# A windowed attention and expert-attention kernel on one core: batch 0 masked on TensorE and loaded in halves, gate steps ordered by data only, set-up work on GpSimd, and a new hand-written order

## The chip, the core and the metric

The kernel runs on one core of a Trainium2 chip. The core has five engines that run their own instruction streams in order and meet at semaphores: TensorE (PE, with a separate stream of weight loads, PEld), VectorE (DVE), ScalarE (ACT), GpSimd (POOL) and SyncE (SP), which here only issues DMAs. The metric is the device time of one execution in microseconds (us). Three runs of the kernel before took 251.45, 252.59 and 254.32 us; the median is 252.59.

## The reference, cut to what matters

There are 8 batches of 576 tokens. Stage one is attention with 8 heads of 64 and a symmetric window of 32 tokens. Its output, with the heads side by side, is x (8 x 576 x 512). Stage two is a mixture of four causal single-head attentions on x, of which each token uses two, with weights from a softmax over the two largest gate logits.

```python
scores = scale * np.matmul(q, k.transpose(0, 1, 3, 2))
mask = np.abs(pos[:, None] - pos[None, :]) <= window
scores = np.where(mask, scores, -1000000000.0)
attn = np.exp(scores - scores.max(-1)); attn /= attn.sum(-1) + 1e-09
x = np.matmul(attn, v)                       # heads side by side: (8, 576, 512)
logits = x @ w_gate                          # 4 experts, the 2 largest kept
for e in range(E):
    q = x @ wq[e]; k = x @ wk[e]; v = x @ wv[e]
    a = causal_softmax(scale * (q @ k.T))
    out += gate[e] * (a @ v @ wo[e])
```

## The kernel before, in words

The whole program is a list of steps, `ORDER`, written out by hand (L25 to L115). A loop at L617 calls the function of each step in turn. A step `name:batch,...#engine@bank` issues its instructions on their engines, so the list fixes the order on every engine at once: PE, DVE, ACT, POOL and the DMA queue of SP each run their own share of the list, in order. `#1` is DVE, `#2` ACT, `#3` POOL, and `@` gives the PSUM banks (0 to 7).

For one batch b, with g the group of four heads, the steps are:

- `lq`, `lk` (L319) load q and k on SP. Part 3 is one DMA for a whole group, each partition holding 18 tokens in a row (`o=18`). Parts 0, 1 and 2 have two tokens per run and four DMAs, one for each head. `lv` (L344) loads V in five tiles of 128 tokens (the last has 64).
- `tq`, `tk` (L336) transpose on DVE.
- `vu`, `vl` (L356) copy V into tiles shifted by 64 tokens, on ACT or POOL.
- `sc` (L366) computes the scores of one group and one half of the columns on PE, in four banks; `ex` (L388) takes the exponential on ACT, two per `sc`; `mk` (L391) multiplies by the 0/1 mask on POOL, one after each `ex`.
- `av` (L398) multiplies by V on PE, and `un` (L418) divides by the row sums on DVE, with a buffer `RC` for the reciprocals. `xt` (L433) transposes x on PE, `xf` (L443) copies it out, `xb` (L453) makes a bf16 copy.
- `ga` (L459) is the gate's matmul. `gt` (L480), `gm` (L489) and `gu` (L497) are its small steps on DVE and `ge` (L486) its exponential on ACT; all four work in one PSUM bank.
- `pp`/`pe` are the q and k projections and their copies, `pv`/`ve` the same for v, `ps`/`xe` the expert scores and their exponentials, `se` the causal selection on POOL, `po`/`oe` the product with v and its scaling, `pt`/`ot` a transpose, `py`/`ye` the output projection, and `st` the store. `ye` and `st` use one of three buffers, chosen by the row tile, so `ye` of the next batch waits for the store of this one.

Set-up steps make the mask (`s_mask`, L239), the identity (`s_ident`), ones and zero paddings (`s_ones`, `s_padx`, `s_pade`, on DVE), load the expert weights (`lw`) and cast them (`cw`, L292, on DVE).

Two rules beyond data order the work. `touch` (L201) makes each instruction on a bank wait for the last instruction of every other engine on that bank, whatever bytes they use. `load` (L230) makes a DMA wait for the last PE instruction that stands before it in the list, so that loads are not begun too early.

## Time and profile before

| | us |
|---|---|
| median of three runs (lowest, highest) | 252.59 (251.45, 254.32) |
| the profiled execution, its own time | 251.16 |
| its span, first to last instruction | 249.50 |
| busy: PE, PEld | 219.0 (88%), 174.7 (70%) |
| busy: DVE, ACT, POOL | 168.6 (68%), 154.0 (62%), 147.2 (59%) |
| chain that ended last: PE, DMA, DVE | 66%, 13%, 11% |
| mean granted TensorE clock | 0.977 |

All durations in this document come from one profiled execution of 251.16 us. "Busy" is the union of an engine's instructions; a matmul's end is modelled, so a busy PE is not PE at its peak. In the timeline, a line gives the start, the length, the engine, the source line, the operation, what it writes and reads, and in brackets how long the engine had been idle before it and what ended that. A line number can be that of a helper: L225 and L224 are the copies on DVE or POOL and on ACT, L231 the loads, L478 the gate's small DVE operations, L328 the transposes of part 3, and L332 those of parts 0 to 2.

### The profile page before, as it was taken

What the parts mean: (1) busy time and instruction counts of PE and PEld (TensorE: products, weight loads), DVE (VectorE), ACT (ScalarE), POOL (GpSimd) and SP (SyncE); (2) the same over time, 40 slices, a digit from 0 to 9 for tenths busy, and PEclk for the clock granted to TensorE, in tenths of its full rate; (3) what the DMA queues carried; (4) which work ended last, traced back from release to release, by engine and by line L of the source; (5) the groups of instructions that cost most, each with busy time, mean ns of one, the idle gap of its engine ahead of it and who ended that gap; (6) DMA issues with size and microseconds to landing.
All of it is one profiled execution on the core that took longest, in us unless ns stands there. A gap on an engine that the chain in (4) does not pass through costs nothing.

```text
span 249.5 us, 12294 instructions
## 1 busy us (share of the span) xinstructions
PE 219.0 (88%) x5474; PEld 174.7 (70%) x5488; DVE 168.6 (68%) x360; ACT 154.0 (62%) x224; POOL 147.2 (59%) x171
## 2 busy tenths in 40 slices
PE   0485897999999999899999999995899999999963
...
PEclk9998899999999999999999999999799999999987
DMA  6995797779895976769936890689032212033166
GB/s 224 210 248 179 192 240 194 170 170 290 185 193 143 202 186 139 247 149 219 247 84 202 198 259 16 174 192 243 1 97 63 83 26 87 4 128 149 52 221 214
DMA packets 71446, 40.66 MB, mean 163 GB/s; under 512 B 46048, under 2 KB 64480, under 8 KB 71392
## 3 DMA queue, kind: packets, MB, share of 16 engines
...
## 4 chain that ended last, share of the span: by engine, by line
PE 66%; DMA 13%; DVE 11%; issue 4%; ACT 2%; SPq 2%; DVEq 0%; ACTq 0%
PE PS L404 13%; PE PS L381 12%; PE PS L516 8%; PE PS L528 7%; PE PS L597 6%; PE PS L437 5%; PE PS L546 5%; PE PS L573 5%; DMA qn<-in_q_dram 5%; DMA V<-in_v_dram 4%; PE PS L462 3%; DMA kn<-in_k_dram 2%; DMA out_dram<-Y 2%; SPq L231 2%; DVE Tkn L328 1%
## 5 line engine op out<-in xcount | busy, mean ns | idle before, releaser
L393 POOL TENSOR_TENSOR A<-A,MASKP 128x576 f32<-128x576 f32 x64 | 89.6, 1419 | 28.3 <-ACT A L389 26.8
L551 ACT ACTIVATE ATE<-PS 128x1024 bf16<-128x1024 f32 (+1 forms) x64 | 51.2, 838 | 23.1 <-PE PS L546 19.9
L389 ACT ACTIVATE A<-PS 128x576 f32<-128x576 f32 x64 | 38.7, 650 | 37.1 <-PE PS L381 36.5
L381 PE MATMUL PS<-Tqn,Tkn 32*64 32x128 f32 (+3 forms) x2560 | 47.8, 284 | 13.9 <-DVE Tkn L328 9.4
L381 PEld LDWEIGHTS PS<-Tqn,Tkn 32*64 32x64 f32 x2560 | 41.0, 140 | 20.2 <-DVE Tkn L328 9.8
L558 POOL TENSOR_SCALAR_AFFINE_SELECT ATE<-ATE 128x384 bf16<-128x384 bf16 (+2 forms) x64 | 26.1, 439 | 26.9 <-ACT ATE L551 26.6
L404 PE MATMUL PS<-V,A 128*64 128x65 f32 x1024 | 36.1, 228 | 3.7 <-POOL A L393 2.0
L404 PEld LDWEIGHTS PS<-V,A 128*64 128x64 f32 x1024 | 33.3, 143 | 7.1 <-POOL A L393 2.1
L225 POOL COPY V<-V 64x2112 f32<-64x2112 f32 (+1 forms) x10 | 18.1, 1813 | 18.7 <-DMA V<-in_v_dram 18.4
L328 DVE STREAM_TRANSPOSE Tqn<-qn 128x576 f32<-128x576 f32 x16 | 19.5, 1246 | 8.2 <-DMA qn<-in_q_dram 8.2
L328 DVE STREAM_TRANSPOSE Tkn<-kn 128x576 f32<-128x576 f32 x16 | 19.8, 1246 | 5.9 <-DMA kn<-in_k_dram 5.9
L423 DVE TENSOR_TENSOR XN<-PS,RC 128x512 f32<-128x512 f32 x32 | 22.1, 692 | 1.1
L597 PE MATMUL PS<-WO,OTT 128*128 128x512 bf16 x66 | 19.0, 409 | 3.3 <-ACT Y L224 1.9
L528 PE MATMUL PS<-WV,XTB 128*128 128x256 bf16 x160 | 21.5, 286 | 0.0
L516 PE MATMUL PS<-XTB,WQ 128*128 128x288 bf16 x128 | 18.0, 286 | 3.5 <-DVE OE L581 3.5
L516 PE MATMUL PS<-XTB,WK 128*128 128x288 bf16 x128 | 18.2, 286 | 0.8 <-DVE WK L295 0.8
L528 PEld LDWEIGHTS <-XTB 128*128 128x128 bf16 x160 | 16.1, 103 | 3.2 <-issue 0.2
L224 ACT CAST QKE<-PS 128x576 bf16<-128x576 f32 x19 | 12.1, 643 | 9.4 <-PE PS L516 9.4
L225 POOL CAST XTB<-XTF 128x128 bf16<-128x128 f32 (+1 forms) x19 | 10.3, 569 | 12.7 <-ACT XTF L224 8.6
L546 PE MATMUL PS<-QKE 64*128 64x64 bf16 (+4 forms) x192 | 17.1, 278 | 0.8 <-DVE QKE L225 0.7
L573 PE MATMUL PS<-VE,ATE 128*128 128x65 bf16 x480 | 17.3, 193 | 0.0
L573 PEld LDWEIGHTS <-ATE 128*128 128x128 bf16 x480 | 16.3, 97 | 1.2 <-POOL ATE L558 0.2
...
## 6 DMA issues: line engine op xcount, KB each, us to landing
...
```

The source lines that it names most:

```text
L225: return (nc.vector if engine == 1 else nc.gpsimd).tensor_copy(out_, in_)
L328: nc.vector.transpose(T.rearrange("q (p o) -> q o p", o=18), n_[:, :].rearrange("p (o d) -> p o d", d=64)[:, :, 32 * dh:32 * dh + 32])
L381: touch(nc.tensor.matmul(one(bank)[64 * par:64 * par + 64, lo - c0:hi - c0], KT[r, dh, k0:k0 + 64], QT[r, dh, lo:hi], start=(dh == 0), sto ...
L389: touch(nc.scalar.activation(a_part(b, g, half, p), two(b0)[:, :, 0:HS], EXP, scale=scale_att), b0, b0 + 1)
L393: nc.gpsimd.tensor_tensor(out=ap, in0=ap, in1=MASK[:, None, HS * half:HS * half + HS].to_broadcast([128, 2, HS]), op=MULT)
L404: touch(nc.tensor.matmul(one(b0 + h // 4)[64 * i:64 * i + 64, 65 * (h % 4):65 * (h % 4) + 65], A[:, h % 4, c:c + 64], V[:, slot, h, 0:65], ...
L516: touch(nc.tensor.matmul(one(b0 + half)[:, 0:HS], WQK[j][n][:, dt, :], XTB[b % 2][:, dt, HS * half:HS * half + HS], start=(dt == 0), stop= ...
L528: touch(nc.tensor.matmul(one(bank)[:, 256 * (t % 2):256 * (t % 2) + 256], XTB[b % 2][:, dt, 128 * t:128 * t + 128], WV[:, dt, :], start=(d ...
L546: touch(nc.tensor.matmul(one(b0 + eo)[:, at:at + hi - lo], Q[r, 1, 128 * kt:128 * kt + 128], Q[r, 0, lo:hi], start=True, stop=True, skip_g ...
L551: touch(nc.scalar.activation(ATE[(2 * b + j) % 3][:, :, 512 * c:512 * c + w], two(b0)[:, :, 0:w], EXP, scale=scale_moe), b0, b0 + 1)
L573: touch(nc.tensor.matmul(one(b0 + eo)[:, 65 * qt:65 * qt + 65], A[:, eo, c:c + 128], V[:, kt, 2 * j + eo, :], start=(kt == 0), stop=(kt == ...
L597: touch(nc.tensor.matmul(one(b0 + i), OTT[b % 2][:, j, 128 * t:128 * t + 128], WO[:, j, :], start=(j == 0), stop=(j == 1)), b0 + i)
```

## The change: what it does

- Batch 0's q and k come in halves: parts 4 and 5 are 9 of the 18 tokens of each partition, one DMA and two transposes for each half and group. Parts 6, 7 and 8 are new shapes with runs of three, six and nine tokens, used for a few later tiles.
- Batch 0's mask moves to PE. `s_maskn` on POOL makes MASKN, which is 0 inside the window and -32768 outside. `mb` puts it into the four score banks by a matmul with the identity (`start=True`), and `sc` then adds the scores to it. Batch 0 has no `mk`; the seven other batches keep theirs.
- `wu` issues four matmuls of zeros, 512 columns wide; it stands three times in the opening and once before batch 0's projections.
- `touch` now adds its wait only where one of the two engines is TensorE. DVE and ACT on one bank are ordered only where one reads or overwrites what the other wrote.
- `s_ones`, `s_padx` and one weight cast go to POOL, one cast to ACT, `s_pade` to a later place. `RC` has four buffers.
- The list is new throughout: another order, other banks, other engines for copies. Apart from batch 0's loads, transposes and masks, each step occurs as often as before.

```diff
-    lq:0,1,3 lk:0,1,3 lk:0,0,0 s_ones s_pade lq:0,0,1 lq:0,0,0 lv:0,1 lv:0,2 lk:0,0,1 tq:0,1,0,3 tk:0,1,0,3
-    tq:0,1,1,3 tk:0,1,1,3 lv:0,0 tq:0,0,0,1 s_mask tk:0,0,1,0 lk:1,0,3 lv:0,4 tq:0,0,1,0 tk:0,0,0,0 s_ident
-    sc:0,1,1@0,2 tq:0,0,0,0 tk:0,0,0,1 ex:0,1,1,0@0 tk:0,0,1,1 ex:0,1,1,1@2 sc:0,0,0@4,6 ex:0,0,0,1@6 lv:0,3
-    tq:0,0,1,1 lq:1,0,3 sc:0,0,1@6,2 ex:0,0,0,0@4 ex:0,0,1,1@2 ex:0,0,1,0@6 tk:1,0,0,3 sc:0,1,0@4,0 mk:0,1,1,1
-    mk:0,0,0,0 lq:1,1,2 mk:0,1,1,0 ex:0,1,0,0@4 vu:0#2 mk:0,0,1,1 mk:0,0,1,0 av:0,3@4 vl:0#2 lk:1,1,2 tk:1,0,1,3
-    mk:0,0,0,1 s_padx lw:0 tq:1,0,1,3 av:0,2@6 lk:2,0,3 tq:1,0,0,3 lv:1,1 mk:0,1,0,0 un:0,2@6 tq:1,1,0,2
-    sc:1,0,0@2,6 ex:0,1,0,1@0 mk:0,1,0,1 un:0,3@4 av:0,1@0 av:0,4@4 ex:1,0,0,0@2 un:0,1@0 un:0,4@4 ex:1,0,0,1@6
-    tq:1,1,1,2 av:0,0@6 lwg un:0,0@6 lw:1 xt:0,2@4 lq:2,0,3 xt:0,1@0 xf:0,2#2@4 sc:1,0,1@4,2 xb:0,2#3
-    ex:1,0,1,0@4 xt:0,0@6 tk:1,1,0,2 ex:1,0,1,1@2 xf:0,1#1@0 mk:1,0,0,0 tk:1,1,1,2 tk:2,0,1,3 cw:0 sc:1,1,1@2,0
...
-    ex:6,1,0,0@2 ex:6,1,0,1@6 xe:4,1,0@4 lv:6,2 tq:7,0,1,3 mk:6,0,1,1 lv:6,1 ps:4,1,1@6 xe:4,1,1@6 ps:4,1,2@2
-    pt:3,0@1 xe:4,1,2@2 gt:5@0 tq:7,0,0,3 mk:6,0,1,0 lq:7,1,2 pp:5,1,1@4 pe:5,1,1#1@4 pp:5,0,0@6 po:3,1@2
-    se:4,0,2 tk:7,1,0,2 pe:5,0,0#2@6 py:2,0@6 vl:6#2 ge:5@0 gm:5@0 oe:3,1@2 pp:5,0,1@4 gu:5@0 pp:5,1,0@2
...
-    xe:7,0,2@2 ge:7@0 py:5,0@2 ve:7,0#2@4 gu:7@0 ot:6,1#1@1 ps:7,0,3@6 po:7,1@4 se:7,0,2 py:6,1@0 xe:7,0,3@6
-    se:7,0,3 st:4,0 ye:5,0#2@2 oe:7,1@4 ye:6,1#2@0 po:7,0@2 st:5,0 st:6,1 py:5,2@4 oe:7,0@2 py:6,0@0 pt:7,1@5
-    ot:7,1#1@5 ye:5,2#2@4 pt:7,0@2 ot:7,0#1@2 st:5,2 ye:6,0#2@0 st:6,0 py:6,2@3 py:7,1@0 ye:6,2#1@3 st:6,2
-    py:7,0@4 ye:7,1#2@0 ye:7,0#2@4 st:7,1 py:7,2@3 ye:7,2#1@3 st:7,0 st:7,2
+    s_zero:#1 lq:0,0,4 lq:0,0,5 tq:0,0,0,4 lk:0,0,5 tq:0,0,1,4 tq:0,0,1,5 tk:0,0,0,5 lq:0,1,5 tk:0,0,1,5 wu:0@0
+    tq:0,0,0,5 lk:0,0,4 tk:0,0,0,4 lk:0,1,4 wu:3@1 lk:0,1,5 s_ident s_mask tk:0,0,1,4 tk:0,1,0,5 lq:0,1,4
+    tq:0,1,1,4 lv:0,3 wu:2@0 lv:0,0 s_maskn mb:0,0,1@0,2 tk:0,1,1,5 lq:1,0,3 mb:0,0,0@4,6 tq:0,1,0,5 tk:0,1,1,4
+    tq:0,1,1,5 lv:0,1 lv:0,2 tk:0,1,0,4 sc:0,0,0@4,6 sc:0,0,1@0,2 tq:0,1,0,4 lv:0,4 lk:1,0,3 s_ones:#3
+    ex:0,0,0,0@4 ex:0,0,1,0@0 lq:1,1,2 mb:0,1,1@4,0 sc:0,1,1@4,0 ex:0,0,0,1@6 tq:1,0,1,3 ex:0,1,1,1@0
+    ex:0,0,1,1@2 mb:0,1,0@6,0 sc:0,1,0@6,0 s_padx:#3 tq:1,0,0,3 ex:0,1,1,0@4 vl:0#2 ex:0,1,0,0@6 lk:1,1,2 vu:0#3
+    ex:0,1,0,1@0 av:0,3@4 tk:1,0,0,3 un:0,3@4 av:0,4@0 tk:1,0,1,3 lv:1,3 av:0,2@6 av:0,0@4 lk:2,0,3 un:0,4@0
+    lw:1 lw:0 sc:1,0,0@2,0 un:0,2@6 av:0,1@6 ex:1,0,0,1@0 xt:0,1@0 ex:1,0,0,0@2 un:0,1@6 lq:2,0,3 sc:1,0,1@2,6
+    xf:0,1#2@0 tk:1,1,1,2 ex:1,0,1,0@2 tq:1,1,1,2 ex:1,0,1,1@6 un:0,0@4 cw:1#2 xb:0,1#2 tq:1,1,0,2 tk:1,1,0,2
+    mk:1,0,0,1 xt:0,0@4 sc:1,1,0@6,2 lv:1,2 ex:1,1,0,1@2 lv:1,1 mk:1,0,0,0 xf:0,0#1@4 tk:2,0,1,3 lv:1,0 xt:0,2@4
+    lv:1,4 lq:2,1,2 xb:0,0#3 mk:1,1,0,1 sc:1,1,1@0,2 xf:0,2#2@4 cw:0#1 wu:1@4 xb:0,2#2 ex:1,1,0,0@6 ex:1,1,1,1@2
+    pp:0,1,1@2 s_pade:#1 tq:2,0,0,3 mk:1,0,1,0 pp:0,1,0@4 pe:0,1,1#2@2 vl:1#3 tk:2,0,0,3 mk:1,1,0,0 ex:1,1,1,0@0
+    mk:1,1,1,0 pe:0,1,0#2@4 tq:2,0,1,3 pp:0,0,1@2 vu:1#2 lwg pp:0,0,0@0 mk:1,0,1,1 mk:1,1,1,1 pe:0,0,0#2@0
+    pe:0,0,1#1@2 sc:2,0,1@4,6 ex:2,0,1,0@4 ex:2,0,1,1@6 av:1,0@2 lk:2,1,2 av:1,1@0 ps:0,0,2@6 ps:0,0,0@4
+    mk:2,0,1,1 un:1,0@2 tq:2,1,0,2 xe:0,0,2@6 ga:0@2 un:1,1@0 xe:0,0,0@4 gt:0@2 sc:2,0,0@6,0 lv:2,1 ex:2,0,0,1@0
...
+    xe:3,0,3@0 lq:7,1,2 mk:5,1,1,1 ve:3,0#2@4 se:2,1,3 gm:4@2 tk:6,0,0,3 po:2,1@0 ye:1,0#2@6 ge:4@2 xb:4,0#3
+    oe:2,1@0 pv:4,0@4 mk:5,0,0,1 pp:4,0,0@0 gu:4@2 lk:7,1,2 se:3,0,2 lv:6,2 mk:5,1,1,0 pe:4,0,0#1@0 ve:4,0#2@4
+    se:3,0,3 sc:5,1,0@2,6 ex:5,1,0,1@6 sc:6,0,0@0,4 pp:4,1,1@6 ex:5,1,0,0@2 vu:5#3 ex:6,0,0,0@0 mk:6,0,0,0
+    tq:6,1,0,2 pe:4,1,1#2@6 pp:4,0,1@0 lk:7,0,3 mk:5,1,0,1 pt:2,1@6 mk:5,1,0,0 pt:2,0@7 tk:6,1,0,2 tq:6,1,1,2
+    ex:6,0,0,1@4 ot:2,1#1@6 pe:4,0,1#2@0 vl:6#2 ot:2,0#1@7 pp:4,1,0@4 po:3,0@6 oe:3,0@6 py:1,1@0 py:2,2@2
...
+    ps:7,0,1@0 xe:7,1,1@4 ga:7@6 ve:7,0#1@2 st:5,1 gt:7@6 pt:6,0@7 ot:6,0#1@7 pt:6,1@4 py:5,0@2 se:7,1,2
+    xe:7,0,1@0 ge:7@6 se:7,0,3 ot:6,1#2@4 po:7,1@0 gm:7@6 py:6,1@4 gu:7@6 se:7,0,2 oe:7,1@0 ye:5,0#2@2 st:5,0
+    ye:6,1#2@4 po:7,0@6 py:5,2@2 oe:7,0@6 py:6,0@4 pt:7,1@3 pt:7,0@6 py:6,2@7 ot:7,1#1@3 ye:5,2#2@2 st:6,1
+    st:5,2 ot:7,0#1@6 py:7,1@2 ye:6,2#1@7 ye:6,0#2@4 st:6,0 st:6,2 ye:7,1#2@2 py:7,2@6 py:7,0@4 ye:7,0#2@4
+    st:7,1 ye:7,2#2@6 st:7,0 st:7,2
...
+    NEGM = -32768.0
...
-    RC = many(2, [128, 2, 4], F32, "RC")
+    RC = many(4, [128, 2, 4], F32, "RC")
...
+    ZERO = sb.tile([128, 512], BF16, name="ZERO")
+    MASKN = sb.tile([128, S], BF16, name="MASKN")
...
+    TENSOR = str(mybir.EngineType.PE)
...
     def regions(ins):
...
-                if other != eng:
+                if other != eng and TENSOR in (other, eng):
...
+    masked = set()
+    def s_maskn():
+        nc.gpsimd.tensor_scalar(out=MASKN, in0=MASK, scalar1=-1.0, scalar2=-NEGM, op0=ADD, op1=MULT)
     def s_warm():
...
-    def s_ones():
+    def at(engine):
+        return nc.vector if engine == 1 else nc.gpsimd
+    def s_zero(engine):
+        at(engine).memset(ZERO, 0.0)
+    def s_ones(engine):
...
-            nc.vector.memset(t[:, :, :, 64:66], 1.0)
-    def s_padx():
+            at(engine).memset(t[:, :, :, 64:66], 1.0)
+    def s_padx(engine):
...
-            nc.vector.memset(t[:, :, S:SP_], 0.0)
-        nc.vector.memset(WG, 0.0)
-    def s_pade():
+            at(engine).memset(t[:, :, S:SP_], 0.0)
+        at(engine).memset(WG, 0.0)
+    def s_pade(engine):
...
-            nc.vector.memset(t[:, :, S:SP_], 0.0)
+            at(engine).memset(t[:, :, S:SP_], 0.0)
...
-            nc.vector.memset(t[:, :, 1600:1664], 0.0)
+            at(engine).memset(t[:, :, 1600:1664], 0.0)
...
-            nc.vector.memset(t[:, :, :, 64:65], 1.0)
-            nc.vector.memset(t[64:128, 4, :, 64:65], 0.0)
+            at(engine).memset(t[:, :, :, 64:65], 1.0)
+            at(engine).memset(t[64:128, 4, :, 64:65], 0.0)
...
-    def cw(n):
+    def cw(n, engine):
...
-                nc.vector.tensor_copy(
-                    WQK[j][n][:, :, :].rearrange("p t (e d) -> p t e d", d=64),
-                    WST[n].rearrange("p (e t d) -> p t e d", t=4, d=64)[:, :, 2 * j:2 * j + 2, :])
+                copy(engine, WQK[j][n][:, :, :].rearrange("p t (e d) -> p t e d", d=64),
+                     WST[n].rearrange("p (e t d) -> p t e d", t=4, d=64)[:, :, 2 * j:2 * j + 2, :])
...
-            nc.vector.tensor_copy(WV[:, :, :].rearrange("p t (e d) -> p t e d", d=64),
-                                  WST[2].rearrange("p (e t d) -> p t e d", t=4, d=64))
-        else:
-            nc.vector.tensor_copy(WO, WST[3].rearrange("p (j x) -> p j x", x=512))
-            nc.vector.memset(ATE[-1][:, :, 1600:1664], 0.0)
-    PART = ((0, 6), (6, 9), (0, 9))
+            copy(engine, WV[:, :, :].rearrange("p t (e d) -> p t e d", d=64),
+                 WST[2].rearrange("p (e t d) -> p t e d", t=4, d=64))
+        else:
+            copy(engine, WO, WST[3].rearrange("p (j x) -> p j x", x=512))
+            at(engine).memset(ATE[-1][:, :, 1600:1664], 0.0)
+    PART = {0: (2, 0, 6), 1: (2, 6, 9), 2: (2, 0, 9), 6: (3, 0, 6), 7: (6, 0, 3), 8: (9, 0, 2)}
+    ROWS = ((0, 18), (0, 9), (9, 18))
     def load_qk(nm, src, b, g, part):
...
-        if part == 3:
-            load(t, src[b, 4 * g:4 * g + 4].rearrange("h (p o) d -> (h p) (o d)", o=18))
+        if 3 <= part < 6:
+            lo, hi = ROWS[part - 3]
+            load(t[:, 64 * lo:64 * hi], src[b, 4 * g:4 * g + 4].rearrange("h (p o) d -> (h p) (o d)", o=18)[
+                :, 64 * lo:64 * hi])
...
-        i0, i1 = PART[part]
+        o, i0, i1 = PART[part]
...
-            load(t[32 * hh:32 * hh + 32, 128 * i0:128 * i1].rearrange("p (i x) -> p i x", x=128),
-                 src[b, 4 * g + hh].rearrange("(i p o) d -> p i (o d)", p=32, o=2)[:, i0:i1, :])
+            load(t[32 * hh:32 * hh + 32, 64 * o * i0:64 * o * i1].rearrange("p (i x) -> p i x", x=64 * o),
+                 src[b, 4 * g + hh].rearrange("(i p o) d -> p i (o d)", p=32, o=o)[:, i0:i1, :])
     def lq(b, g, part):
...
     def turn(nm, b, g, dh, part):
...
-        if part == 3:
-            nc.vector.transpose(T.rearrange("q (p o) -> q o p", o=18),
-                                n_[:, :].rearrange("p (o d) -> p o d", d=64)[:, :, 32 * dh:32 * dh + 32])
+        if 3 <= part < 6:
+            lo, hi = ROWS[part - 3]
+            nc.vector.transpose(T.rearrange("q (p o) -> q o p", o=18)[:, lo:hi],
+                                n_[:, :].rearrange("p (o d) -> p o d", d=64)[:, lo:hi, 32 * dh:32 * dh + 32])
...
-        i0, i1 = PART[part]
+        o, i0, i1 = PART[part]
...
-            T[:, 64 * i0:64 * i1].rearrange("q (i p o) -> q i o p", p=32, o=2),
-            n_[:, 128 * i0:128 * i1].rearrange("p (i o d) -> p i o d", o=2, d=64)[:, :, :, 32 * dh:32 * dh + 32])
+            T[:, 32 * o * i0:32 * o * i1].rearrange("q (i p o) -> q i o p", p=32, o=o),
+            n_[:, 64 * o * i0:64 * o * i1].rearrange("p (i o d) -> p i o d", o=o, d=64)[:, :, :, 32 * dh:32 * dh + 32])
     def tq(b, g, dh, part):
...
+    def mb(b, g, half, b0, b1):
+        masked.add((b, g, half))
+        for bank in (b0, b0 + 1, b1, b1 + 1):
+            touch(nc.tensor.matmul(one(bank)[:, 0:HS], ident_bf, MASKN[:, HS * half:HS * half + HS],
+                                   start=True, stop=False, skip_group_check=True), bank)
+    def wu(i, b0):
+        for _ in range(4):
+            touch(nc.tensor.matmul(one(b0), ZERO[:, 0:128], ZERO, start=True, stop=True), b0)
     def sc(b, g, half, b0, b1):
+        first = (b, g, half) not in masked
...
-                                       start=(dh == 0), stop=(dh == 1), skip_group_check=True), bank)
+                                       start=(first and dh == 0), stop=(dh == 1), skip_group_check=True), bank)
     def a_part(b, g, half, p):
...
     def un(b, T, b0):
...
-            rc = RC[T % 2]
+            rc = RC[T]
...
```

## The prediction

> **What bounds the kernel now.** I read the page's slices first, then busy time by stretch, then the timeline of the two stretches where TensorE (PE) is not full.
>
> ```profile
> PE   0485897999999999899999999995899999999963
> ...
> PEclk9998899999999999999999999999799999999987
> DMA  6995797779895976769936890689032212033166
> ```
>
> PE is full (9) from about 50 us to 230 us, but for one dent in slice 28 (168 to 175 us). It is not full in the first 50 us and at the end. The clock row dips at the same three places.
>
> ```profile
> 0.00:10.00 10.00, 0.73 (x16) 0.33 (x16) 5.59 (x16) 1.28 (x1) 4.57 (x14) 1.00 0.77 213
> 10.00:20.00 10.00, 8.42 (x302) 7.46 (x304) 3.39 (x10) 3.58 (x6) 4.78 (x4) 1.00 1.08 254
> 20.00:30.00 10.00, 6.40 (x189) 5.75 (x175) 7.41 (x13) 5.28 (x6) 6.32 (x5) 0.83 0.60 155
> 30.00:40.00 10.00, 8.66 (x338) 7.40 (x335) 9.40 (x14) 4.88 (x10) 5.85 (x6) 1.00 0.91 230
> 40.00:50.00 10.00, 8.86 (x184) 6.29 (x182) 8.13 (x19) 6.67 (x11) 9.20 (x6) 1.00 0.80 185
> 50.00:80.00 30.00, 29.09 (x822) 23.80 (x824) 23.22 (x51) 23.22 (x34) 17.80 (x20) 1.00 0.85 196
> ```
>
> The columns after the length are PE, PE weight load, DVE, ACT, POOL, PE clock, DMA share, GB/s. In the first 50 us PE lacks 17 us; later 30 us lack 1.
>
> The head's timeline shows what it waits for:
>
> ```profile
> 12.70 2.28 PE L381 MATMUL PS<-Tqn,Tkn 32*64 32x64 f32 x80 [0.62 <-DVE Tqn L332]
> ...
> 21.36 3.49 ACT L224 COPY V<-V 64x2112 f32<-64x2112 f32 x2 [0.45 <-DMA V<-in_v_dram]
> ...
> 23.37 3.53 PE L404 MATMUL PS<-V,A 128*64 128x65 f32 x62 [0.81 <-ACT V L224]
> ```
>
> Batch 0's scores (`sc`) wait for the transposes. Its `av` waits for V, whose last tile lands at 21.36, and for the copies of V.
>
> The dent:
>
> ```profile
> 171.88 1.51 ACT L224 COPY V<-V 64x1584 f32<-64x1584 f32 x1 [1.91 <-DMA V<-in_v_dram]
> ...
> 173.29 0.18 ACT L487 ACTIVATE EX<-PS 128x20 f32<-128x20 f32 x1
> ...
> 173.50 0.18 DVE L478 TENSOR_TENSOR GE<-PS,m 128x20 f32<-128x20 f32 x1 [3.64 <-ACT EX L487]
> ...
> 174.69 0.82 DVE L581 TENSOR_TENSOR OE<-PS,RG 128x640 bf16<-128x640 f32 x1
> ...
> 175.58 1.15 PE L516 MATMUL PS<-XTB,WQ 128*128 128x288 bf16 x8 [3.52 <-DVE OE L581]
> ```
>
> Here `vl:6` on ACT waits for V. The gate's exponential `ge` stands behind it, DVE's `gm` waits for `ge`, `oe` stands behind `gm`, and PE's bank is freed by `oe`.
>
> **A ruler.** Full-speed PE lengths from the stretch where PE is full: `sc` 1.27 (96 in two: 2.46 in the chain), `av` 1.02 (four: 4.10), `av` tile 4 0.59, `xt` 0.87, `pp` 0.98, `pv` 1.75 + 0.44, `ga` 1.22, `po` 0.91, `ps` 0.43, `pt` 0.28, `py` 0.85. The old list sums to 209.8 us. Time minus the sum so far I call the lag. From the timeline it is 15.1 when batch 0's scores are done (20.2), 21.0 after its `av` (32.0), 24.4 at 54.9, 26.8 at 171.9, 31.9 after the dent (188.5), 31.0 at 232.5, 35.3 at PE's end (245.1); then 4.4 for the last copy and store. So the head costs 24.4, the dent 5.0 and the tail 8.7; the whole rest costs 2.
>
> **The change, part by part.** The sum is made against the profiled execution: 251.16 us, span 249.50. The median of the three runs is 1.43 above it.
>
> *Warm-up and mask on PE.* 16 matmuls of 512 columns, at 0.40 cold (ten took 4.01 us at 241) and 0.21 warm, are 3.4 to 6.4 us; 16 of 288 columns at 0.123 (`pp`: 8 in 0.98) are 2.0, or twice that cold. Twelve of the former run before 7 us, when PE has nothing else: before, its first `sc` started at 7.93. The other four stand before `pp:0,1,1`, where PE waits for ACT and DVE. I take 0. Without the cover it is 0.85 to 1.6 at `wu:1`, and 0.5 to 1.0 for each of the two `mb` behind `ex`.
>
> *Does the warm-up pay?* `sc` took 2.28 us at 12.70 and 1.36 at 55.95. So a warm start saves about 0.9 on each of the two first `sc`. But the third `sc` waits for DVE, so the sum takes 0.
> [...]
>
> *POOL.* The mask multiply `mk` falls away 8 times, 8 x 1.42 = 11.4 us. Mask and identity ended at 5.62; the new `s_maskn` on 576 columns costs between 0.6 (cast of 1024: 1.04) and 1.42 (`mk`). I take 0.7, since it has one input: 6.3. `mb` is then done by 8, ahead of the transposes. The moved memsets are 165 to 272 ns each on DVE; POOL's own took 0.21 (128x128) and 0.63 (128x640), so six are 1 to 2.5 us, between 7 and 20 us, where POOL now does nothing. 0.
>
> *The loads of batch 0.* Each half is 295 KB and one issue (0.40 to 0.46 us). Those behind `wu:0` and `wu:3` wait for PE until about 3 and 5 us. In the old rates (2.13 MB in the first 10 us, 254 GB/s after), group 0's four halves land by about 7.7. DVE's transposes of half a tile are taken as 0.63, half of 1246 ns. Group 0 is ready at 9.1, all of q and k at 15.3. PE: `sc:0,0,0` and `sc:0,0,1` 9.1 to 12, `sc:0,1,1` 15.3, `sc:0,1,0` to 19. Up to `lv:0,2` the queue moves 3.97 MB: 17.2, plus 2 to 3.4 to land (the old `lv:0,3` stood at 4.13 MB, 17.9, and landed at 21.36). I take 20.0.
> Then `vl:0` on ACT and `vu:0` on POOL (1.5, 1.95): `av:0,3` starts at 22.0, against 23.37. No `mk` stands in the way; the old ones ran until 24.9 and 26.9.
> On DVE `un:0,3` now stands behind `tk:1,0,0,3`, thus behind `lk:1,0,3`, at 4.69 MB: 20.1 + 2.5 = 22.6. So `un:0,3` ends at 24.8, `un:0,4` 26.6, `sc:1,0,0` 28.0, `sc:1,0,1` 31.3 (old: 34.6), `xt:0,0` 33.3 (old: 35.7), `sc:1,1,0` 35.3. Then ACT and DVE decide: `cw:1` on ACT (2, from DVE's 1.96), `xb`, four `ex`, and on DVE `xf`, a transpose of 1.25 and `cw:0` (2.64) to 39.1. The four `pp` end near 44, `sc:2,0,1` at 45.4 (old: `pp:0,0,1` at 47.7 after the same work), `sc:2,0,0` at 51. The new list has done 27.4 us of ruler by then: lag 23.4, against 24.4. The lead of 3 us shrinks to 1: the second 15 us of ruler hold 14.5 of DVE, 15.7 of ACT and 13.9 of POOL, so all four engines are full. **Term: -1.0**, bounds -4.0 (the lead is kept) and +2.5 (a tenth less DMA rate delays V of batch 1 by 4).
>
> *Gate ordered by data.* DVE's `gm` no longer waits for `ge`. The waits list has 6.0 us in 4 waits; only the 3.64 reached PE. `vl:6` is on ACT in the new list too. `lv:6,2` stands behind the four issues of `lk:7,1,2` (such groups took 1.8 to 4.2), which wait for `pp:4,0,0`: issued 2.3 after it, landed at 7.2 (median 4.9). ACT reaches `vl:6` at about 5.4, ends it at 8.7, and `pe:4,1,0` behind it at 9.5. PE's cover (`pp`, two `pt`, `pp`, `po`, two `py`) ends at 8.2. So 1.3 lost where 5.0 was: **-3.7**, bounds -5.0 (V in time) and +1.0 (issues 4.2, landing 6.2: 4.4, plus 1.6 of slow clock as in 170 to 200, clock 0.94).
>
> *The new list elsewhere.* Work per engine by rows: DVE 180 to 171, ACT 166 to 172, POOL 146 to 137, PE +5.4 in covered places. In cuts of 15 us of ruler the fullest is 90 to 105: ACT 15.2, POOL 14.6, against 13.3 and 12.9 in the old list's second half. The old stage with 14.4 and 14.4 took 17.6 us instead of 15. I take **+1.2**, bounds 0 and +3.
>
> *Tail.* Both lists have the same 7.1 us of PE work after `py:5,0`, and the same chain of `ye:5,0`, `st:5,0`, `ye:6,0`, `st:6,0`, `ye:7,0`, `st:7,0` through one buffer (235.2 to 249.5): 0, between -0.7 and +0.7.
>
> Sum: -1.0 - 3.7 + 1.2 = -3.5: 251.16 - 3.5 = 247.7.
>
> **The rivals.**
> - *The new list's waits eat the gain.* The ACT wait at `vl:6` is as dear as the old one and the crowded stage costs 3: -1.0 + 0 + 3 is 253.2; with either alone, 249.5 to 251.4. I put it at 251.4. For it: three full engines at 30 and 90 to 105. Against it: `gm` and `oe` are off that chain. Chance 0.20.
> - *Slower: batch 0's normalisation waits for batch 1's k.* `un:0,3` stands behind `lk:1,0,3`. The old `lq:1,0,3` took 7.5 us to land (15.51 to 23.0). Each us beyond 22.6 costs one; to be slower than before it must land after 26. At 28 it is +5.4, plus 1.7 for a clock of 0.83 over 10 us: 254.8. Against it: the queue is in order and holds only 4.69 MB. Chance 0.17.
> - *The head keeps its lead.* -4.0, no wait at `vl:6` (-5.0), +1.2: 243.4. For it: less DVE and POOL work. Against it: ACT's 15.7. Chance 0.14.
>
> **How the numbers follow.** The forecast, 247.7 (its own range 245 to 250), has 0.49. One per cent, 2.5 us, is about what a measurement of this kernel can tell from no change. Faster is the forecast and the early case, 0.63; within 1% the eaten gain, 0.20; slower the late k, 0.17. The range goes from the early case to the late one with a little cut from either: 243.5 to 254.0.
>
> **What would show it.** Right: first `sc` near 9, `av:0,3` near 22, lag 23 to 24 near 51; no DVE wait for `ge`; a PE gap of 1 to 2 us before `ps:4,1,0`. Wrong: DVE idle before a `tk` of batch 1 past 26 us, `mb` waiting for POOL, PE idle between 100 and 130 us behind ACT's exponentials, or a tail longer than 14.3 us from `st:5,0`.

## The result, and the profile after

| | before | changed |
|---|---|---|
| median of 20 runs each, same chip (us) | 253.27 (251.27 to 256.92) | 253.15 (248.14 to 260.98) |
| ratio to before, 95% interval | | 0.9878 [0.9834, 0.9922] |
| the same ratio on another occasion (12 and 35 runs) | | 0.9947 [0.9888, 1.0005] |
| profiled execution: its time, span | 251.16, 249.50 | 253.3, 251.6 |

By the ratios the gain is 0.5 to 1%, by the medians nothing: it is at the edge of what can be told from none. The ratios use only the executions within 1.5% of a kernel's own fastest (6 of the changed kernel's 20, 16 of before's), while the medians use all, and the changed kernel spreads more. Note also that the profiled execution of before is 2.1 us shorter than its median and the changed kernel's is at its median, so the pair of profiles, read alone, says 2.1 us slower.

The slices of the changed kernel's page (40 slices of 6.3 us):

```profile
PE   6777888959997899999779999899999999999991
...
PEclk9979999988999999999958999999999999999998
DMA  6959999377678768666803599524810543042066
```

The dent of slice 28 (counted from one) is gone. There is a new one in slices 20 and 21 (120 to 132 us), with a clock dip in slices 21 and 22, and others in slices 9 and 13. The old head, 0 4 8 5, is now 6 7 7 7.

Busy time by stretch in the changed kernel (PE, PE weight load, DVE, ACT, POOL, PE clock, DMA share, GB/s):

```profile
0.00:10.00 10.00, 6.46 (x84) 3.14 (x91) 5.67 (x10) 1.28 (x1) 6.37 (x21) 1.00 0.83 267
10.00:20.00 10.00, 7.42 (x285) 5.13 (x273) 6.47 (x10) 5.13 (x8) 1.59 (x1) 0.83 0.76 185
20.00:30.00 10.00, 8.12 (x263) 7.13 (x271) 6.16 (x12) 2.96 (x5) 2.42 (x3) 1.00 1.19 259
30.00:40.00 10.00, 9.02 (x264) 6.85 (x265) 9.41 (x21) 7.20 (x16) 4.97 (x5) 1.00 1.00 229
40.00:50.00 10.00, 9.29 (x308) 7.70 (x306) 4.10 (x10) 6.97 (x9) 8.20 (x7) 1.00 0.66 126
50.00:80.00 30.00, 25.43 (x651) 21.47 (x647) 23.51 (x51) 18.87 (x28) 18.04 (x19) 0.94 0.74 192
```

The first row's PE is mostly warm-up (the twelve `wu`, 4.14 of the 6.46 us). The last row is the surprise: from 50 to 80 us PE had 29.09 and now has 25.43.

The changed head on the timeline (start, length, engine, line, operation, what it writes and reads; in brackets the idle time before and what ended it):

```profile
8.76 2.87 PE L416 MATMUL PS<-Tqn,Tkn 32*64 32x64 f32 x160 [1.32 <-DVE Tkn L349]
...
14.28 2.34 PE L416 MATMUL PS<-Tqn,Tkn 32*64 32x64 f32 x80 [1.48 <-DVE Tqn L349]
...
18.41 1.94 POOL L231 COPY V<-V 64x2112 f32<-64x2112 f32 x1 [10.96 <-DMA V<-in_v_dram]
...
20.40 1.15 PE L439 MATMUL PS<-V,A 128*64 128x65 f32 x30 [0.88 <-POOL V L231]
21.99 1.26 DVE L349 STREAM_TRANSPOSE Tkn<-kn 128x576 f32<-128x576 f32 x1 [3.22 <-DMA kn<-in_k_dram]
```

Two `sc` take 2.87 us together, at a granted clock of 1.00; the third, after 1.48 us of idle time, takes 2.34, and the clock reads 0.51 from 14.28 to 16.62. V's copy runs at 18.4, and `av:0,3` at 20.4 instead of 23.37.

**The lag** (end of a step on PE minus the ruler's sum up to it, as in the prediction; "h2" is the last experiment below):

| at the end of | before | changed | a1 | g1 | h1 | h2 |
|---|---|---|---|---|---|---|
| `sc:0,1,0` | 15.2 | 14.2 | 13.2 | 15.7 | 14.0 | 14.4 |
| the four `pp` of batch 0 | 24.6 | 21.0 | 22.9 | 26.6 | 21.5 | 21.6 |
| `av:1,4` | 24.4 | 22.9 | 24.1 | 26.4 | 23.0 | 22.0 |
| `pp:1,1,1` (66 to 69 us) | 25.5 | 26.6 | 26.4 | 27.8 | 26.7 | 26.1 |
| `po:2,0` (121 to 125 us) | 27.2 | 28.9 | 29.4 | 30.7 | 28.6 | 28.2 |
| `av:5,2` (154 to 165 us) | 27.2 | 35.9 | 36.1 | 30.9 | 31.0 | 29.6 |
| `av:6,4` (181 to 193 us) | 32.2 | 35.1 | 35.7 | 31.8 | 30.6 | 28.9 |
| `pv:7,0` | 31.2 | 35.6 | 36.3 | 30.8 | 30.8 | 29.2 |
| span | 249.5 | 251.6 | 252.4 | 248.9 | 246.8 | 245.5 |

So the head kept 3.6 us up to batch 0's projections and 1.5 at `av:1,4`; then the new list lost 3.4 between 53 and 59 us, some 2.5 between 72 and 90, 4.6 at 123 to 130 and 1.6 more by 134; from `av:1,4` to 154 us the old list's lag grew by 2.8 in all. Of the 2.5, some 1.4 come from a wait for `oe:0,1`, which stands on DVE behind transposes that waited 2.38 for k, and 0.9 from a stop of PE by itself (0.87 at 83.09; last section).

The loss at 53 to 59 us, the gate of batch 0 (L528 and L542 are `gm` on DVE, L537 is `ge` on ACT, L601 `xe`, L487 `xt`):

```profile
54.78 0.19 DVE L528 TENSOR_TENSOR PS<-PS,m 128x20 f32<-128x20 f32 x1
55.00 0.19 ACT L537 ACTIVATE EX<-PS 128x20 f32<-128x20 f32 x1 [3.47 <-DVE PS L528]
...
55.08 1.19 ACT L601 ACTIVATE ATE<-PS 128x128 bf16<-128x128 f32 x2
...
55.41 3.54 PE L487 MATMUL PS<-ident,XN 128*128 128x128 f32 x16 [1.61 <-ACT ATE L601]
```

ACT stood for 3.47 us with `ge:0`, which reads nothing that `gm:0` writes, until `gm:0` had done its last operation on the same bank. `gm:0` stood on DVE behind normalisations. `xe:0,0,3` behind `ge:0` held the bank that PE needed, and PE then ran 16 transposes in 3.54 us (8 took 1.09 at 84.3 us, where the granted clock reads 1.00): the clock reads 0.50 from 55.3 to 58.6 us.

The loss at 123 to 130 us (L353 a transpose; L528, L550, L551 the gate's `gu:3`; L629 to L631 `oe:2,0`):

```profile
123.66 0.33 PE L416 MATMUL PS<-Tqn,Tkn 32*64 32x64 f32 x4
...
125.30 1.21 DVE L353 STREAM_TRANSPOSE Tqn<-qn 128x576 f32<-128x576 f32 x1 [4.53 <-DMA qn<-in_q_dram]
126.37 0.22 DVE L528 TENSOR_TENSOR PS<-EX,PS 128x20 f32<-128x20 f32 x1
...
127.08 0.19 DVE L528 TENSOR_TENSOR G<-PS,su 128x20 f32<-128x20 f32 x1
...
127.33 2.25 PE L416 MATMUL PS<-Tqn,Tkn 32*64 32x64 f32 x76 [3.33 <-DVE G L528]
```

DVE waits 4.53 us at `tq:5,1,1,8` for a load that batch 5 needs much later. Behind it stands `gu:3`, which frees the bank of `sc:5,0,1`; PE waits 3.33 and comes back at half clock (0.50 from 127.0 to 133.7 us).

At the old dent's place the changed kernel has this:

```profile
158.24 1.51 ACT L230 COPY V<-V 64x1584 f32<-64x1584 f32 x1 [1.60 <-DMA V<-in_v_dram]
...
160.34 0.61 PE L596 MATMUL PS<-QKE 64*128 64x512 bf16 x4 [0.79 <-ACT QKE L230]
```

`vl:6` still waits for V, and PE for the copy behind it, before `ps:4,1,0`, as the prediction said; it loses 0.79 us (1.53 in a1), where 1.3 was put down.

### The profile page after: what moved, and what is told of

Its sections match the earlier page's. It is cut to its first block, busy times and chain, and to the rows that moved or that the text cites. A ratio compares the mean times of both kernels' runs of the same rounds, so it can differ in the third digit from the quotient of the medians.

```text
span 251.6 us, 12333 instructions
## 1 busy us (share of the span) xinstructions
PE 224.1 (89%) x5507; PEld 176.6 (70%) x5520; DVE 165.3 (66%) x347; ACT 158.1 (63%) x237; POOL 140.1 (56%) x169
## 4 chain that ended last, share of the span: by engine, by line
PE 54%; DMA 20%; DVE 12%; SPq 5%; issue 5%; ACT 2%; DVEq 0%; ACTq 0%
PE PS L439 10%; DMA kn<-in_k_dram 9%; PE PS L416 9%; PE PS L566 6%; PE PS L487 6%; SPq L237 5%; PE PS L596 5%; DMA qn<-in_q_dram 5%; DMA V<-in_v_dram 4%; PE PS L647 4%; PE PS L578 4%; PE PS L623 3%; PE PS L512 3%; DVE Tqn L353 2%; DMA out_dram<-Y 2%
## 5 line engine op out<-in xcount | busy, mean ns | idle before, releaser
L428 POOL TENSOR_TENSOR A<-A,MASKP 128x576 f32<-128x576 f32 x56 | 78.2, 1416 | 25.7 <-ACT A L424 25.5
L601 ACT ACTIVATE ATE<-PS 128x1024 bf16<-128x1024 f32 (+1 forms) x64 | 50.9, 837 | 19.3 <-PE PS L596 18.0
L416 PE MATMUL PS<-Tqn,Tkn 32*64 32x128 f32 (+3 forms) x2560 | 45.9, 276 | 7.7 <-DVE G L528 3.3
L416 PEld LDWEIGHTS PS<-Tqn,Tkn 32*64 32x64 f32 x2560 | 39.5, 135 | 14.1 <-DVE G L528 3.5
L608 POOL TENSOR_SCALAR_AFFINE_SELECT ATE<-ATE 128x384 bf16<-128x384 bf16 (+2 forms) x64 | 26.1, 439 | 29.5 <-ACT ATE L601 29.3
L439 PE MATMUL PS<-V,A 128*64 128x65 f32 x1024 | 36.3, 229 | 3.3 <-POOL V L231 0.9
L349 DVE STREAM_TRANSPOSE Tkn<-kn 128x576 f32<-128x576 f32 (+1 forms) x22 | 22.8, 1050 | 6.3 <-DMA kn<-in_k_dram 4.1
L231 POOL CAST XTB<-XTF 128x1024 bf16<-128x1024 f32 (+1 forms) x16 | 12.4, 791 | 25.1 <-DVE XTF L231 16.8
L349 DVE STREAM_TRANSPOSE Tqn<-qn 128x576 f32<-128x576 f32 (+1 forms) x22 | 22.5, 1049 | 5.0 <-DMA qn<-in_q_dram 4.7
L230 ACT CAST QKE<-PS 128x576 bf16<-128x576 f32 x24 | 15.2, 640 | 9.0 <-PE PS L566 8.1
L578 PE MATMUL PS<-WV,XTB 128*128 128x256 bf16 x160 | 20.2, 273 | 0.6 <-DVE OE L631 0.6
L487 PE MATMUL PS<-ident,XN 128*128 128x128 f32 x128 | 18.3, 294 | 1.7 <-ACT ATE L601 1.6
L647 PE MATMUL PS<-WO,OTT 128*128 128x512 bf16 x68 | 17.6, 379 | 1.4 <-DVE OTT L231 0.4
L230 ACT COPY Y<-PS 128x1024 f32<-128x1024 f32 (+1 forms) x18 | 15.1, 846 | 4.5 <-PE PS L647 3.6
```

The source lines that it names most:

```text
L230: return nc.scalar.copy(out_, in_)
L231: return (nc.vector if engine == 1 else nc.gpsimd).tensor_copy(out_, in_)
L349: nc.vector.transpose(T.rearrange("q (p o) -> q o p", o=18)[:, lo:hi], n_[:, :].rearrange("p (o d) -> p o d", d=64)[:, lo:hi, 32 * dh:32 * ...
L416: touch(nc.tensor.matmul(one(bank)[64 * par:64 * par + 64, lo - c0:hi - c0], KT[r, dh, k0:k0 + 64], QT[r, dh, lo:hi], start=(first and dh ...
L428: nc.gpsimd.tensor_tensor(out=ap, in0=ap, in1=MASK[:, None, HS * half:HS * half + HS].to_broadcast([128, 2, HS]), op=MULT)
L439: touch(nc.tensor.matmul(one(b0 + h // 4)[64 * i:64 * i + 64, 65 * (h % 4):65 * (h % 4) + 65], A[:, h % 4, c:c + 64], V[:, slot, h, 0:65], ...
```

## The experiments

Each time stands beside runs of the kernel before on the same chip. Where an experiment's list is wrapped anew, its lines stand four or so lower than the changed kernel's (`sc` is L412, not L416).

### The three losses, and the list's order (a1, b1, c1, d1)

a1 is the changed kernel again.

> The changed kernel once more, for a second profile and for times beside the kernel before. In its first profile the lag (time minus the ruler's sum) was 20.9 us at sc:2,0,1, 22.8 after av:1,4, 26.2 after xt:1,2, 28.9 at sc:3,1,1, 33.3 after sc:5,0,1 and 35.5 at pv:7,0. Theory: the three rises (3.4 at the gate of batch 0, 2.5 at 72 to 90 us, 4.5 at the gate of batch 3) are made by the order of the list and come again within 1 us each; the ratio to before is 0.985 to 1.0. Rival: they come from that execution's memory transfers; then at least one of them is gone.

b1 puts the gate's exponential first, so that it no longer waits for `gm:0`:

```diff
-    gt:0@2 sc:2,0,0@6,0
+    gt:0@2 ge:0@2 sc:2,0,0@6,0
...
-    un:1,2@6 gm:0@2 ge:0@2 xe:0,0,3@0
+    un:1,2@6 gm:0@2 xe:0,0,3@0
```

> One step moved: ge:0 right after gt:0, ahead of gm:0, instead of after it. Theory: in the changed list ge:0 on ACT waits for gm:0 on DVE, because DVE and ACT on one bank still follow the list, and gm:0 stands behind two normalisations; xe:0,0,3 behind ge:0 holds the bank of xt:1,0. Then ACT's wait of 3.5 us before EX goes, the lag after xt:1,2 falls from 26.2 to 23 or 24, and the time falls by 2 to 3 us if nothing later takes it back. Rival: xt:1,0 waits for DVE's normalisations anyway; then less than 1 us.

c1 puts `gu:3` ahead of the transpose that waits for its load:

```diff
-    mk:4,0,0,0 tq:5,1,1,8 se:2,0,2
+    mk:4,0,0,0 gu:3@2 tq:5,1,1,8 se:2,0,2
...
-    po:2,0@0 gu:3@2 ps:2,1,0@4
+    po:2,0@0 ps:2,1,0@4
```

> One step moved: gu:3 ahead of the transpose tq:5,1,1,8 on DVE. Theory: that transpose waits for its load (landed at 125.3), gu:3 stands behind it, and sc:5,0,1 needs the bank that gu:3 frees; PE lost 3.3 us and some slow clock. Then PE's gap before the 76 matmuls is under 0.5 us, the lag at sc:5,0,1 falls from 33.3 to about 29, and the time by 3.3 to 4.8 us. Rival: oe:2,0 on DVE stands behind the same transpose and PE stops a little later for tq:5,1,0 or oe; then 0 to 2 us.

d1 is both.

> Both moves, ge:0 ahead of gm:0 and gu:3 ahead of tq:5,1,1,8. Theory: the two gains add, 5 to 7 us, 245 to 247 us in the undisturbed runs. Rival: PE only reaches the next late load earlier and gives half of it back; then 2 to 4 us.

Before had a median of 255.18. Medians and ratios: a1 253.37, 0.9947 [0.9888, 1.0005]; b1 252.79, 0.9986 [0.9924, 1.0047]; c1 253.38, 0.9913 [0.9844, 0.9982]; d1 252.22, 0.9926 [0.9879, 0.9973]. The first theory held in the main: the rises recur in a1, though not all within 1 us (2.0 at 60 us, where 3.4 was; 4.3 in two steps at 128 to 130), and those at 72 to 90 us stand at other steps (one is PE's wait of 1.53 at 84.8 for ACT, which waits for the cast of a late weight load). The gains of b1, c1 and d1 did not come; none of the three can be told from a1. In b1 the wait itself went, and the lag after `xt:1,2` is 23.8 instead of 26.0 to 26.3. But it rises by 0.9 at `sc:2,1,0`, a stop of PE by itself (0.74 at 58.99; last section), and by 1.5 at `pv:0,1`, where PE waits 1.32 for the weight cast `cw:2`: at `pp:1,1,1` it is 26.4, as in a1. In d1 it is 23.7 there, but 28.6 at `po:2,0` and 35.2 at `pv:7,0`. In c1 the wait passed on to the next step behind it:

```profile
122.84 1.22 DVE L349 STREAM_TRANSPOSE Tqn<-qn 128x576 f32<-128x576 f32 x1 [3.61 <-DMA qn<-in_q_dram]
...
125.39 0.82 DVE L627 TENSOR_TENSOR OE<-PS,RG 128x640 bf16<-128x640 f32 x1
...
126.27 0.61 PE L592 MATMUL PS<-QKE 64*128 64x512 bf16 x2 [3.69 <-DVE OE L627]
```

`oe:2,0` stands behind the same transposes, and `ps:3,1,0` needs its bank. Its rise is 3.9, against 4.3 in a1. One step was taken from behind the wait, and the next one was late.

### The wait moved as a whole (h1)

```diff
-    mk:4,0,0,0 tq:5,1,1,8 se:2,0,2
+    mk:4,0,0,0 se:2,0,2
...
-    ps:2,1,0@4 tk:5,1,1,7 ot:1,0#2@3 lv:5,1 pe:3,1,1#2@6 oe:2,0@0 sc:5,0,1@6,2
+    ps:2,1,0@4 ot:1,0#2@3 lv:5,1 pe:3,1,1#2@6 oe:2,0@0 tq:5,1,1,8 tk:5,1,1,7 sc:5,0,1@6,2
```

> The changed list with two steps moved: the transposes tq:5,1,1,8 and tk:5,1,1,7, which wait on DVE for late loads, now stand behind oe:2,0. Theory (one late load, three steps behind it): in c1 the gate's gu:3 went ahead of the wait, and the wait passed to oe:2,0 and so to PE's bank for ps:3,1,0, where the lag still rose by 3.9. With both behind oe:2,0 the rise at sc:5,0,1 and ps:3,1,0 (4.3 to 5.5 in the five profiles with the list's own order) is under 1 us, and PE's lag at ps:2,1,2 is 29 to 31 instead of 33.4 to 35.1. Time: 2 to 4 us shorter than the changed kernel. Rival (the loads come no earlier, so PE meets the next late one): the rise comes back at av:4,x, at ps:4,1,0 (V of batch 6) or at pp:6,1,1, the lag at PE's end is again above 35, and the time is less than 1.5 us shorter.

250.84 beside 254.43, ratio 0.9851 [0.9791, 0.9911]. The same place in h1:

```profile
123.64 0.82 DVE L627 TENSOR_TENSOR OE<-PS,RG 128x640 bf16<-128x640 f32 x1
124.61 0.39 PE L592 MATMUL PS<-QKE 64*128 64x512 bf16 x2
...
124.89 1.28 DVE L349 STREAM_TRANSPOSE Tqn<-qn 128x576 f32<-128x576 f32 x1 [0.43 <-DMA qn<-in_q_dram]
...
129.07 0.39 PE L592 MATMUL PS<-QKE 64*128 64x512 bf16 x2 [1.31 <-DVE XN L454]
```

The load lands when it did (124.9, against 125.3), but of what PE needs only batch 4's normalisation now stands behind it, and PE waits 1.31 for that. From `po:2,0` to `av:5,2` the lag rises by 2.4 instead of 7.0; it is 4.9 lower there and stays so to the end (30.8 at `pv:7,0` against 35.6). In the profile that is 4.8 us of span; the ratio is 0.3 to 1.0% below the changed kernel's two, and the intervals leave between nothing and 2%. In the profile the theory stands and the rival does not: what this place no longer loses is not lost later. The times alone (0.7 to 2.4 us) do not decide between the theory's 2 to 4 us and the rival's less than 1.5.

### The dent of the kernel before (g1)

```diff
-    py:2,0@6 vl:6#2 ge:5@0 gm:5@0
+    py:2,0@6 ge:5@0 vl:6#2 gm:5@0
```

> The kernel before with one step moved: vl:6 on ACT now stands behind the gate's exponential ge:5, and nothing else is changed. Theory (the dent of the kernel before is the chain V, vl:6, ge:5, gm:5, oe:3,1, pp:5,0,1): DVE's wait of 3.64 us for the exponential and PE's of 3.52 for oe go; PE waits for ACT's copies behind vl:6 instead, at most 1.5 us; the lag, which rose by 5.0 in the old dent, rises by 0 to 2. Time: 2 to 4 us shorter than before. Rival (the late V keeps PE waiting through the copies pe:5 behind vl:6): the rise stays 4 or more and the time is the same within 1 us. Second rival (the time is given back at a later load): the rise goes, but the lag at the end of PE is again above 34.5, and the time is less than 1 us shorter.

249.81 beside 254.60, ratio 0.9853 [0.9796, 0.9910]. In g1 (L484 is `ge:5`, L475 `gm:5`, L578 `oe:3,1`):

```profile
173.71 0.19 ACT L484 ACTIVATE EX<-PS 128x20 f32<-128x20 f32 x1
...
173.94 0.18 DVE L475 TENSOR_TENSOR GE<-PS,m 128x20 f32<-128x20 f32 x1 [0.23 <-ACT EX L484]
...
175.13 0.82 DVE L578 TENSOR_TENSOR OE<-PS,RG 128x640 bf16<-128x640 f32 x1
...
175.97 1.51 ACT L221 COPY V<-V 64x1584 f32<-64x1584 f32 x1 [2.07 <-DMA V<-in_v_dram]
...
176.01 1.15 PE L513 MATMUL PS<-XTB,WQ 128*128 128x288 bf16 x8
```

V is as late as before (2.07 of wait, against 1.91), but only copies stand behind it. DVE's wait for the exponential is 0.23 instead of 3.64, and PE's only stop here is 0.63 us at 178.1, for a copy on ACT behind `vl:6`. One step moved by one place in the old list is worth as much as the whole change. `touch` is the old one here.

### The head, one part at a time (e1, f1, k1, i1)

e1 leaves the warm-up out of the changed list:

```diff
-    tk:0,0,1,5 wu:0@0 tq:0,0,0,5
+    tk:0,0,1,5 tq:0,0,0,5
...
-    cw:0#1 wu:1@4 xb:0,2#2
+    cw:0#1 xb:0,2#2
```

(and `wu:3`, `wu:2` likewise)

> The changed list without the four steps of warm-up; they have no part in the output. Theory (the warm-up buys nothing that lasts): the first two sc take 2.3 us each instead of 1.4, so they end about 1.5 to 1.9 us later than 11.63, but the third sc still waits for the last transpose of batch 0's q on DVE, which stood at 14.2: sc:0,1,0 ends within 0.7 us of the 16.8 to 18.0 of the five profiles with warm-up. Before batch 0's projections wu:1 adds 0.85 (four matmuls), and in all five profiles the lag rises by 1.0 at pp:0,1,1; without it that rise is 0.3 or less. Time: 0 to 1 us shorter than the changed kernel. Rival (a warm start pays): sc:0,1,0 ends 1.5 to 2 us later, and the time is 1 to 2 us longer.

256.90 beside 254.60, ratio 0.9981 [0.9919, 1.0042], so 0.3 to 1.0% above the changed kernel's two ratios, with intervals that overlap those of a1. In e1:

```profile
9.13 4.53 PE L412 MATMUL PS<-Tqn,Tkn 32*64 32x64 f32 x160 [0.77 <-DVE Tkn L345]
...
14.79 1.02 PE L412 MATMUL PS<-Tqn,Tkn 32*64 32x64 f32 x51
...
18.67 1.36 PE L412 MATMUL PS<-Tqn,Tkn 32*64 32x64 f32 x80
```

Without warm-up the first pair takes 4.53, not 2.87 (the granted clock reads 1.00 from 0 to 20 us), but the third `sc`, from 14.79, does its first 51 matmuls in 1.02; with warm-up the first pair is done early, PE then has only two short mask steps in 2.65 us, and the third `sc` takes 2.34 from 14.28, at a granted clock of 0.51. The warm-up mostly moves the slow `sc`. The last score step ends at 20.0 instead of 19.3; the five profiles with warm-up have 18.0 to 19.8 (the 16.8 to 18.0 of the expectation are about where the step starts). One number of the expectation fell: the rise of 1.0 at `pp:0,1,1` is still there without `wu:1`, so that step had stood in a wait and had cost nothing. Whether the warm-up is worth some tenths of a per cent stays open.

f1 puts the mask of batch 0 back on GpSimd:

```diff
-    s_maskn mb:0,0,1@0,2 tk:0,1,1,5 lq:1,0,3 mb:0,0,0@4,6
+    s_maskn tk:0,1,1,5 lq:1,0,3
...
-    ex:0,0,0,0@4 ex:0,0,1,0@0
+    ex:0,0,0,0@4 mk:0,0,0,0 ex:0,0,1,0@0 mk:0,0,1,0
```

> The changed list with batch 0 masked on GpSimd as before (eight multiplies, one behind each exponential), and no mask on PE. Theory (the mask on PE is what brings av:0,3 forward): eight multiplies of 1.42 us are 11.4 us of GpSimd between 11.2 and about 24; vu:0 stands behind six of them and starts at 20.5 to 22 instead of 18.4, the last multiply ends at 23 to 25, and av:0,3 starts 3 to 5 us later than its 19 to 20.4. PE has four mb fewer (0.5 each). At pp:0,0,0 2 to 4 us are left of it, and 1 to 3 us in the time, since later waits give part of it back. Rival (DVE's wait for lk:1,0,3 until 21 to 23 us sets the pace anyway): av:0,3 is late but pp:0,0,0 ends within 1 us of the 39.8 to 43.6 of the five profiles, and the time is the same within 0.7 us.

261.72 beside 254.60, ratio 1.0273 [1.0202, 1.0345]. In f1 (L425 is `mk`, L228 `vu:0`):

```profile
20.95 2.75 POOL L425 TENSOR_TENSOR A<-A,MASKP 128x576 f32<-128x576 f32 x2
23.77 1.94 POOL L228 COPY V<-V 64x2112 f32<-64x2112 f32 x1
25.76 2.00 PE L436 MATMUL PS<-V,A 128*64 128x65 f32 x30 [5.80 <-POOL V L228]
```

`vu:0` waits behind seven multiplies and four memsets, and PE runs from 10 to 20 and from 20 to 30 us at a clock of 0.67 and 0.50; the lag is 26.2 at the four `pp` (21.0 with `mb`) and 42.9 at `pv:7,0` (35.6). The theory's mechanism held; its 1 to 3 us were too few (7.3 of lag, and 3.3 to 4.0% by the ratios), for nothing was given back and the gate of batch 0 lost 4.6 this time.

k1 loads batch 0's q and k whole:

```diff
-    s_zero:#1 lq:0,0,4 lq:0,0,5 tq:0,0,0,4 lk:0,0,5 tq:0,0,1,4
+    s_zero:#1 lq:0,0,3 tq:0,0,0,4 lk:0,0,3 tq:0,0,1,4
```

(and group 1 likewise)

> The changed list with batch 0's q and k loaded whole (one DMA for a group, 590 KB, four issues instead of eight), the transposes still in halves. Theory (the halves start DVE earlier): the first transpose starts about 1.2 us later than 3.68 (295 KB more at 254 GB/s), and since DVE then works through sixteen transposes of 0.55 to 0.7 us each, the first sc starts 0.5 to 1.5 us later than 8.8 and the last transpose ends 0.5 to 1.2 us later than 14.2; V lands at most 0.5 us earlier. Left in the time: 0 to 1 us longer. Rival (the issues are what V waits for): with four issues of 0.4 us fewer V of batch 0 lands 1 us or more earlier, av:0,3 starts earlier than 19, and the time is 0.5 to 1.5 us shorter.

256.30 beside 254.60, ratio 1.0097 [1.0048, 1.0146]. But not for the reason expected:

```profile
4.59 1.80 DVE L345 STREAM_TRANSPOSE Tqn<-qn 128x288 f32<-128x288 f32 x3 [3.39 <-DMA qn<-in_q_dram]
...
8.60 2.87 PE L412 MATMUL PS<-Tqn,Tkn 32*64 32x64 f32 x160 [1.18 <-DVE Tkn L345]
...
16.83 1.43 PE L412 MATMUL PS<-Tqn,Tkn 32*64 32x128 f32 x41 [2.50 <-issue]
```

The first transpose starts 0.9 later, but the first `sc` 0.16 earlier, and V's copy on POOL 1.9 earlier (16.54), as the rival had it, without its gain. In this profile the head's loss (a lag of 25.2 at the four `pp`) comes mostly from PE stopping for 2.50 us in the middle of an `sc`, with no engine to wait for (last section), and three times more by 38 us, 5.6 in all. Whether whole loads bring about more of such stops was not tried, so why the halves pay stays open.

i1 is the old list, with nothing of the change's steps but the mask on PE (`RC` has its four buffers here too; only DVE uses it):

```diff
-    s_ident sc:0,1,1@0,2
+    s_ident s_maskn mb:0,1,1@0,2 sc:0,1,1@0,2
...
-    sc:0,1,0@4,0 mk:0,1,1,1 mk:0,0,0,0 lq:1,1,2 mk:0,1,1,0
+    mb:0,1,0@4,0 sc:0,1,0@4,0 lq:1,1,2
```

> The old list with one part of the change: batch 0 is masked on PE (MASKN and four mb, each ahead of its sc) and not on GpSimd. Loads, order and engines of all other steps are the old ones. Theory (in the old list V sets batch 0's av, not the mask): av:0,3 still waits for V and its copy on ACT and starts at 22 to 23.4, but the later av no longer wait for multiplies that ended at 24.9 and 26.9, so the lag behind batch 0's av falls from 21.0 to 18.5 to 20.5; 0.5 to 2 us are left in the time. Rival (the mask is worth as much here as in the changed list, where putting it back cost 7 us): 4 us or more shorter. Second rival (PE's own mb are in the way, 0.5 to 1.0 each before a cold sc): no gain.

256.27 beside 254.43, ratio 1.0028 [0.9972, 1.0083]: no gain. The lag behind batch 0's `av` is 23.0 in i1's profile, an execution of 260.28 us, and 20.1 in i2's, which has the same head; with the old mask it is 21.1 in before and 22.9 in g1. Executions with the same head differ by 2 to 3 us, and the mask is lost in that. In the old list `vu:0` and `vl:0` are on ACT and wait for V, not for multiplies. So the mask on PE is worth 7 us or more in the new list and nothing that could be measured in the old. By f1's rows it pays because the new list puts `vu:0` on the engine that it frees; the new list with `vu:0` on ACT and the old mask was not tried.

i2 is i1 and g1 together.

> i1 and g1 together: the old list, batch 0 masked on PE, and vl:6 behind ge:5. Theory (two stalls 130 us apart add up): g1's 3.5 to 4.8 and i1's 0.5 to 2 are 4 to 7 us shorter than the kernel before, and no rise over 1 us is left between 165 and 190. Rival (what the head gains is given back at the loads of the middle, as in the changed list): no shorter than g1 alone, within 1 us.

250.48 beside 254.43, ratio 0.9770 [0.9688, 0.9851], against g1's 0.9853 [0.9796, 0.9910]. The ratio is 0.8% below g1's, the median, held against before's, 0.3% above: whether the two add up stays open.

### Six edits of the new list (h2)

```diff
-    av:0,3@4 tk:1,0,0,3 un:0,3@4 av:0,4@0
+    av:0,3@4 un:0,3@4 tk:1,0,0,3 av:0,4@0
...
-    vl:6#2 ot:2,0#1@7
+    ot:2,0#1@7
...
-    pe:4,1,0#2@4
+    pe:4,1,0#2@4 vl:6#2
```

(with h1's two transposes, b1's `ge:0`, no `wu:1`, and `lw:3` ahead of `lv:2,4`)

> The changed list with six edits: the two transposes of h1 moved; un:0,3 ahead of tk:1,0,0,3; ge:0 right behind gt:0; wu:1 left out (it has no part in the output); vl:6 behind pe:4,1,0 on ACT; and the load lw:3 ahead of lv:2,4. Theory (each removes one wait that the profiles show, and they add up in part): 2 to 4 from the transposes, about 1 from DVE's wait for lk:1,0,3 (3.2 to 4.3 us, of which un:0,3 lost 1.5), 1 to 2 from the gate of batch 0, 0.8 to 1.7 from vl:6, 1 to 1.5 from the POOL cast that waits 4 to 5.5 us for lw:3, and nothing from wu:1. 6 to 10 in all on paper; 4 to 6 us shorter than the changed kernel, since the loads come no earlier. Rival (the DMA queue sets the pace): 0 to 2 us shorter, with PE's gaps at other loads.

247.36 beside 254.43, ratio 0.9690 [0.9626, 0.9754]: the quickest of all, 5 to 7 us below the changed kernel by the ratios (0.988 and 0.995) and by the medians (0.972 of before's, against 0.993 and 1.000), where 4 to 6 were expected. What each of the six is worth was not tried, but for h1. Its lag at `pv:7,0` is 29.2, where before has 31.2. `un:0,3` and `vl:6` no longer delay PE; of the 59 us gate 2.5 came back at `pv:0,1`. The slices of its page:

```profile
PE   7759778986997899999979999999999999999980
```

From slice 22 on (129 us) PE is full, but for the last two.

## Why the prediction came out as it did

The number, 247.7 from 251.16 (a ratio of 0.986), agrees with the first ratio (0.988) and less with the second (0.995). The medians moved by 0.1 us, and 253.15 is inside the wide range but outside the forecast's own (245 to 250). In the pair of profiles the change is +2.1, not -3.5. The sum is made of terms that were wrong in both directions, so where the number agrees it is in good part luck.

- *Warm-up and mask on PE, 0.* Right: twelve `wu` run from 1.26 to 5.4 (the first seven start 0.40 to 0.43 us apart, those from 4.15 on 0.22), `wu:1` stood in a wait (e1), and two of the four masks took 1.14 together. The "third `sc` waits for DVE" happened too: it started at 14.28 (15.3 predicted), and at a granted clock of 0.51.
- *POOL, 0.* MASKN ended at 6.25 (6.3 predicted). What was not priced is what f1 shows: seven multiplies ahead of `vu:0` would have cost 7 or more.
- *Head, -1.0.* `lk:1,0,3` landed at 21.99 (22.6), `sc:1,0,1` ended at 31.2 (31.3), but the four `pp` at 41.7 (44) and the lag near 50 us was 21.7 (23.4). The mis-sized step is "`cw:1` on ACT (2 ...) and `cw:0` (2.64)": they took 1.14 and 0.76. In the kernel before, both casts on DVE ran beside a multiply on POOL; in g1, which has the same order here, the second one (WK) did not. First before, then g1:

```profile
36.34 2.95 POOL L393 TENSOR_TENSOR A<-A,MASKP 128x576 f32<-128x576 f32 x2
36.94 2.64 DVE L295 CAST WQ<-Y 128x512 bf16<-128x512 f32 x2
...
40.59 1.96 DVE L295 CAST WK<-Y 128x512 bf16<-128x512 f32 x2
```

```profile
42.46 0.73 DVE L292 CAST WK<-Y 128x512 bf16<-128x512 f32 x2
...
43.97 2.78 POOL L390 TENSOR_TENSOR A<-A,MASKP 128x576 f32<-128x576 f32 x2 [2.81 <-ACT A L386]
```

The same cast of WK took 1.96 beside a multiply and 0.73 without one. The 2.64 too was the price of a cast beside a multiply, and the new list pays such a price elsewhere: `cw:2` took 1.56 us beside a multiply, and in a1, where it came first, 0.69, while POOL's cast took 1.56 instead of 1.04. Why these took longer is not shown. At `av:1,4` the lead was 1.5, close to the 1.0.
- *Gate ordered by data, -3.7.* The size nearly came true (-4.7), the reason is false. The dent went (5.3 before, 0.6 to 0.8 now; 1.9 at most in the other profiles), because the new list has no gate behind `vl:6`; g1 does the same by moving one step. "DVE's `gm` no longer waits for `ge`" fell: with the old `touch` put back the changed kernel is the same program, instruction for instruction, so DVE and ACT on one bank are not ordered by data alone after the change either. The framework already keeps the engines that use one bank in the order of the list, whether or not they share bytes, and the 3.47 us of `ge:0` behind `gm:0` show it at work. The gate's order on two engines was a new cost, not a saving.
- *New list elsewhere, +1.2.* This is the step that failed. From `av:1,4` to the old dent's place the old list's lag grows by 2.5 (24.4 to 26.9) and the new one's by 12.5 (22.9 to 35.4). It was sized by full engines ("the fullest is 90 to 105", counted in ruler: 119 to 140 us here). That stretch lost the most, 6.1 (28.8 to 34.9), but not because its engines were full. First the changed kernel, then h1, in the same columns as above:

```profile
120.00:125.00 5.00, 3.99 (x60) 3.17 (x57) 0.43 (x1) 3.94 (x6) 4.17 (x4) 1.00 0.80 215
```

```profile
120.00:125.00 5.00, 5.00 (x137) 4.01 (x136) 2.52 (x9) 3.76 (x7) 4.22 (x4) 1.00 0.79 226
```

DVE is busy for 0.43 of these 5 us: it stands still for one load. In h1, with the same work and only two transposes moved, the whole stretch lost 1.5 (28.4 to 29.9). So what the new list lost came from single waits in queues: a gate in list order (3.4), one late load with `gu:3` and `oe:2,0` behind it (6.2 with the slow clock after it), and at 72 to 90 us `oe:0,1` behind a late k and a stop of PE by itself (2.5; in a1 such a stop and a late weight load). Reading for each wait what stands behind it is the step that would have found all but PE's own stops. Of the rivals, "the new list's waits eat the gain" came nearest: it named this stretch, but priced it by full engines, and its other part, a wait at `vl:6` as dear as the old one, cost 0.8. Its sum of 253.2 agrees with the median of 253.15 in the number and not in the cause.
- *Tail, 0.* It gained 2.3: in both, 16.8 us pass from the end of `pv:7,0` to the end of the span, but the new list has 10.6 us of ruler left there and the old one 8.3. The last ten matmuls of `py`, before and after:

```profile
241.09 4.01 PE L597 MATMUL PS<-WO,OTT 128*128 128x512 bf16 x10 [1.93 <-ACT Y L224]
```

```profile
243.70 2.32 PE L647 MATMUL PS<-WO,OTT 128*128 128x512 bf16 x10 [0.43 <-DVE OTT L231]
```

The old ones came after a wait for the store, and the granted clock reads 0.50 from 241.6 to 244.9 us; the new order has work in front, PE was idle for 0.43 before them, and the clock reads 1.00 from 243 to 247. "The same 7.1 us of PE work" was true of the work and not of the clock.
- *The slower rival* (late k of batch 1) is a real wait: DVE stood 3.2 to 4.3 us for it in five profiles, with landings at 20.6 to 23.1, before the 26 from which it decides.

In the pair of profiles: -1.5 (head) + 10.0 (list) - 4.7 (dent, 5.3 to 0.6) + 0.6 (from there to `pv:7,0`) - 2.3 (tail) = +2.1, which is the difference of the spans.
